# Turning one pair's queries with a DMA transpose and emitting that pair's scores later

## The chip, the cores and the metric

The kernel runs on one core of one Trainium2 chip. The metric is the device time of one execution in microseconds (us); three runs of the kernel before took 225.99, 226.20 and 226.31 us, so the median is 226.2 us.

A core has five engines that run their own instruction streams and wait for each other by semaphores: TensorE (PE in the profile, with its weight loads as PEld), VectorE (DVE), ScalarE (ACT), GpSimd (POOL) and SyncE (SP), which here only issues DMA. TensorE writes to eight banks of PSUM, each of 128 partitions by 512 float32.

## The reference, cut to what matters

```python
def _attn_ref(q, k, v, is_retrieval, n_sink, window):        # 4 batches, 8 heads, 768 tokens, 64 wide
    scores = scale * np.matmul(q, k.transpose(0, 1, 3, 2))
    ...
    stream_keep = causal & (is_sink | in_win)                # 4 sinks, window of 64
    mask = np.where(retr, causal, stream_keep)               # heads 0, 2 and 6: causal; the others: windowed
    a = softmax(np.where(mask, scores, -1e9))
    return np.matmul(a, v)

def reference(...):
    x = attn_out.transpose(0, 2, 1, 3).reshape(B * S, H * D) # 3072 tokens, 512 wide
    h = x @ w_in                                             # 512 x 2048
    g = np.maximum(h, 0.0) + alpha * np.minimum(h, 0.0)
    return g @ w_out                                         # 2048 x 512
```

## The kernel before, in words

**Tiles.** The heads go in four pairs per batch, `PAIRS = [(2, 6), (1, 5), (0, 4), (3, 7)]`, and the pairs of all batches are numbered n = 0 to 15; batch 1 has 4 to 7. Pair 4 has two full heads (`RETR`), pairs 5 and 7 two windowed ones, pair 6 one of each (head 0 full, head 4 windowed). Each pair's queries lie transposed in `qT` (64 rows for each head of the pair, 768 columns), its keys in `kT`.

**Steps.** Everything the kernel does is cut into named steps, and one table, `ORDER`, gives the order in which they are emitted; each engine runs its own steps in that order. The names:

- `Lq`, `Lk`, `Lv` n: loads of a pair from DRAM, issued by SP. `Cq`, `Ck`, `Cv`: casts to bf16 on ACT, DVE or POOL.
- `Tq`, `Tk` n: six 128x128 transposes on TensorE into a bank (L377); `tq`, `tk`: their copies out of PSUM, on ACT (L382 for the queries).
- `Dq`, `Dk` n: the same turn as a DMA transpose issued by SP (L335 for queries); before, only for pairs 8 to 15.
- `S`n.h.m: the scores of piece m of head h (0 or 1) of pair n. A full head has six pieces of 448 columns, a windowed one three of 352, 352 and 448. `s`: the exponential on ACT (L485 full, L557 and L559 windowed), which frees the bank. `m`: the mask on DVE.
- `A`n.h: probabilities times values on TensorE (L595); `a`: division on DVE (L605, L606). `X`n: the pair's output turned into `xT` by a DMA transpose on SP (L614).
- `P`t.f: the first matmul of a stretch t of tokens (L640); `p`, `g`: its activation on ACT and DVE. `O`t.s.u: a quarter (four matmuls, L660) of the second; `o`: its copy out on ACT (L666) and its store from POOL. Stretches 0 and 1 are batch 0, 2 and 3 batch 1, so that batch 0's second matmul runs while batch 1's attention does.
- `near`i: resets of a buffer for windowed probabilities, on DVE.

**Scores side by side.** From pair 4 on, `S` steps are only collected, in `burst`, and `emit_burst` writes them out when the next step comes that isn't allowed beside them (`beside_burst`). If both halves (first heads and second heads) have at least `SPLIT = 576` columns, matmuls of the two halves are interleaved, each on its own 64 rows of the array (L446), and run at the same time. If not, they go one behind the other on all 128 rows (L439).

**Banks.** `take` gives a step the bank that was freed longest ago in the order of emission, `give` returns it. The choice is fixed when the program is written; when the program runs, TensorE waits until that bank has really been read out.

**DMA.** SP's DMAs run in order on one queue, and each waits for a semaphore that the eighth one before it used. The rows of `q` are loaded with `row_tokens(n)` tokens in a piece: 6 for n < 8, so that one load brings 128 x 2 rows of 1536 bytes (L212), and 1 from n = 8 on, which makes two loads of 128 x 6 rows of 256 bytes (L215). With 6 the columns come out of the transpose permuted, and `put_q` puts them in order while it copies; the DMA transpose can't, and needs 1.

Of the kernel before, what the change touches and what calls it, by code (L numbers as in the profile page):

```python
# [34 lines left out]
m6.1.1 s7.1.2 m6.1.0 s7.0.2 m7.0.2 S6.0.4 S6.0.2 S4.1.2 S6.1.2 S6.0.0 s4.1.2 s6.0.4 m4.1.1 s6.0.1 s6.1.2 O1.0.1 m6.0.5
m7.1.0 m4.1.4 m7.1.2 m6.1.2 S6.0.3 A4.1 s6.0.0 m6.0.0 m6.0.1 A7.1 O1.1.2 A6.1 s6.0.3 m6.0.4 m6.0.3 s6.0.2 a4.1 a6.1
A6.0 A7.0 a6.0 O1.1.3 O0.0.0 O0.0.1 O0.0.2 O1.0.2 m10.0.2 O1.0.3 O0.0.3 o0.0 X4 X6 a7.1 a7.0 X7 P2.9 P2.3 p2.9 P3.4
Ck9 Cq9 g2.9 P2.14 p2.14 g2.14 Cq8 p3.4 Lq10 Lq11 Dk8.0 P2.10 p2.10 Dk9.1 o1.0 p2.3 g2.3 g3.4 Dk8.1 P3.2 P3.14 P3.12
P2.8 Dq8 P2.1 P3.8 o1.1 p3.2 Dk9.0 Lv10 g2.10 Dq9 p3.14 P2.7 Ck10 g3.2 p3.12 g3.12 g3.14 P2.2 p2.2 g2.2 Cq10 Dq10
P2.11 p2.1 g2.1 p2.11 p2.8 g2.11 P3.6 P2.5 p2.5 g2.5 P2.13 p2.13 g2.8 g2.13 P2.0 p2.0 g2.0 p2.7 P3.0 p3.0 P2.4 S8.0.5  # L40
Lv8 Lv11 P2.15 P2.12 s8.0.5 Cq11 g3.0 p2.15 g2.7 g2.15 S8.0.0 p2.12 g2.12 Ck11 p3.6 P2.6 s8.0.0 p2.6 S9.0.2 g3.6 p2.4
g2.4 s9.0.2 g2.6 p3.8 P3.10 g3.8 p3.10 O3.0.0 O2.0.0 S8.1.5 s8.1.5 O3.0.1 O2.0.1 g3.10 m8.0.0 Cv8 S8.1.3 S9.0.0 S8.0.3
S8.0.1 S9.1.0 s8.1.3 s9.1.0 s8.0.1 s9.0.0 s8.0.3 m8.0.3 m8.0.1 O2.0.2 O2.0.3 o2.0 Dk10.1 Lv9 m9.0.0 Cv9 m8.0.5 Dk11.0
m9.1.0 m9.0.2 S8.0.4 S9.1.1 S9.0.1 S8.1.4 S10.1.1 Dq11 s9.1.1 s8.1.4 Lq13 Lk13 O3.0.2 Dk10.0 s10.1.1 s9.0.1 s8.0.4
O3.0.3 o3.0 Dk11.1 S10.1.0 S10.1.2 m9.0.1 S11.0.2 S9.1.2 S8.0.2 S11.0.0 s9.1.2 Cv10 m9.1.1 A9.0 s11.0.2 s10.1.0 O2.3.0
m9.1.2 A9.1 a9.0 a9.1 X9 s10.1.2 s11.0.0 O2.3.1 Lq15 Lv14 Lq12 S8.1.0 S11.0.1 m10.1.0 s8.0.2 S10.0.1 S8.1.2 S10.0.3
S8.1.1 S10.0.0 O2.3.2 s8.1.2 s8.1.0 m8.1.4 Cq13 s11.0.1 s8.1.1 m11.0.2 m8.0.4 m11.0.0 A8.0 s10.0.0 m8.1.5 m10.1.1
O2.3.3 m10.1.2 a8.0 S11.1.2 S10.0.4 S11.1.0 S10.0.2 S10.0.5 m8.1.3 m11.0.1 s10.0.3 s10.0.1 S11.1.1 s10.0.2 s11.1.2
A10.1 s11.1.1 O2.2.0 O2.1.0 s10.0.4 m6.0.2 m10.0.1 Cv11 m8.1.1 m8.1.0 a10.1 m10.0.4 Ck13 m10.0.0 m11.1.2 A11.0 A8.1
O2.1.1 s10.0.5 o2.3 s11.1.0 Dk13.0 m11.1.1 m10.0.3 m10.0.5 m11.1.0 A10.0 a11.0 a8.1 a10.0 O3.1.0 A11.1 Cq12 O2.2.1  # L50
O2.2.2 O2.2.3 a11.1 X8 O2.1.2 O3.1.1 O3.1.2 X10 o2.2 O3.1.3 O2.1.3 X11 P4.11 o2.1 P4.14 P5.14 p5.14 P4.4 P4.6 Lk12
P5.0 g5.14 Ck12 p4.4 p4.6 p4.11 P4.13 g4.6 p4.14 g4.11 Lq14 g4.14 P5.12 P4.5 P4.12 p4.13 Dq12 o3.1 p5.0 g4.13 Cq14
g5.0 Dk13.1 p4.5 g4.5 g4.4 Cv14 P4.9 p4.9 g4.9 P4.2 P5.2 Dq13 p5.12 g5.12 P4.10 p5.2 P4.8 P4.1 p4.12 g4.12 g5.2 p4.10
g4.10 Lv15 Dk12.0 Dk12.1 Lv12 p4.1 Lk14 Lv13 Lk15 g4.1 P4.7 P4.0 p4.2 g4.2 p4.8 g4.8 p4.0 p4.7 g4.7 P4.15 S12.0.5 Cv12
S13.0.1 s13.0.1 S12.0.3 s12.0.5 P4.3 s12.0.3 P5.4 g4.0 p4.3 S12.1.5 S12.0.1 S12.0.0 S13.1.1 s13.1.1 Dq14 g4.3 Cq15
Ck14 m12.0.3 O4.3.0 s12.1.5 s12.0.1 O4.3.1 O4.3.2 s12.0.0 p4.15 g4.15 P5.6 P5.10 S12.1.1 S12.0.4 S12.0.2 p5.4 S13.1.0
g5.4 p5.6 s12.0.4 Dk14.0 P5.8 s13.1.0 s12.0.2 p5.8 s12.1.1 m12.0.0 g5.6 O4.3.3 Ck15 p5.10 g5.8 m12.0.1 g5.10 m12.0.4
O5.1.0 Cv13 O5.1.1 O5.1.2 o4.3 Dk14.1 S14.1.1 S14.0.0 S12.1.4 S14.0.1 S14.1.0 S13.0.2 m12.1.1 s14.1.0 s13.0.2 O4.2.0
m12.0.5 A12.0 s14.0.1 s12.1.4 O5.1.3 Dk15.1 s14.1.1 Dk15.0 s14.0.0 a12.0 m14.0.1 Dq15 o5.1 O4.2.1 S13.1.2 S12.1.2
S14.1.2 S14.0.4 m13.1.0 m14.0.0 m13.0.1 S14.0.5 S13.0.0 O4.2.2 O4.2.3 s13.1.2 m13.1.2 m13.1.1 s13.0.0 s14.0.4 s14.0.5  # L60
m13.0.2 S12.1.0 m12.1.5 s14.1.2 S12.1.3 S15.0.0 S14.0.3 m13.0.0 A13.1 o4.2 s12.1.0 s12.1.2 A13.0 s15.0.0 O5.0.0
s12.1.3 s14.0.3 m14.0.4 Cv15 a13.1 O5.0.1 a13.0 S15.0.1 S15.0.2 m12.1.0 S15.1.0 S15.1.2 S15.1.1 S14.0.2 O4.1.0 s15.0.2
s15.1.0 m12.1.4 s14.0.2 s15.1.1 m14.1.1 m14.0.5 m14.1.2 m12.1.3 m14.1.0 A12.1 m14.0.3 A14.1 A14.0 s15.1.2 m15.0.0
m15.0.2 m15.1.0 s15.0.1 m15.1.1 O4.1.1 X13 m15.1.2 m15.0.1 a14.0 a14.1 A15.0 A15.1 a12.1 O4.0.0 X14 O4.0.1 O4.0.2
O4.0.3 X12 o4.0 a15.0 O4.1.2 a15.1 O4.1.3 X15 o4.1 O5.0.2 O5.0.3 o5.0 P6.11 p6.11 P6.2 P6.15 P6.10 p6.10 P7.4 P6.0
P6.1 g6.11 g6.10 p6.1 P6.6 P7.8 p6.15 g6.15 g6.1 p6.0 g6.0 P6.5 p7.4 p6.5 p6.6 g7.4 g6.6 g6.5 P6.3 P6.12 P7.2 p6.3
p6.12 g6.12 p6.2 g6.2 P6.4 p7.8 P7.6 P6.14 g6.3 g7.8 p7.6 p6.4 g7.6 g6.4 P7.10 P6.7 P6.8 p6.8 p6.7 P7.0 P6.9 P6.13
g6.7 p7.2 g7.2 g6.8 p7.10 g7.10 p6.9 P7.14 O6.3.0 P7.12 p6.13 g6.13 p7.12 O6.0.0 O6.0.1 O6.1.0 p7.0 g7.0 g6.9 O6.3.1
O7.0.0 O6.3.2 O6.1.1 p7.14 p6.14 g6.14 g7.12 O6.3.3 o6.3 O6.0.2 O6.1.2 O6.1.3 o6.1 O6.0.3 o6.0 O6.2.0 O6.2.1 O6.2.2
# [5 lines left out]
def kernel(  # L75
# [293 lines left out]
    def to_array(key, nat, choices, first_half=False):  # L369

        held[key] = take(*choices)
        tr = bank_bf(held[key][0])
        for i in range(6):
            if first_half:
                nc.tensor.transpose(tr[0:D, 128 * i:128 * (i + 1)], nat[:, i, 0:D], ident)
            else:
                nc.tensor.transpose(tr[:, 128 * i:128 * (i + 1)], nat[:, i, :], ident)  # L377
# [520 lines left out]
```

## Time and profile before

| | |
|---|---|
| median of 3 runs | 226.2 us (225.99 to 226.31) |
| profiled execution, its own time | 226.88 us |
| its span, first to last instruction | 225.2 us |
| granted TensorE clock | 1.000 |
| batch 1's scores and sums | about 56.7 to 74.3 us |
| first matmul of batch 1 begins | 80.3 us |
| HBM read, written | 27.71 MB, 6.29 MB |

A group's line on the page names the line of the program, the engine, the operation, what it writes and reads, the count, busy time and mean; behind the second bar stands the idle time of the engine just before, with what ended most of it. The chain that ended last is followed back from the last instruction: at each step to what released it, or to the instruction before it on its engine. In its order of time a row is start, length and what ran. In the timeline a row is start, length, engine, line and operation, with the engine's idle time before it in brackets. SPq rows are the issue of a DMA on SP, not its transfer.

### The profile page before, as it was taken

To read this page: it belongs to the slowest core of one execution; us is meant where nothing else is said; L and a number is where in the kernel's file an instruction comes from. 1 tells how busy PE (TensorE), PEld (TensorE's weight loads), DVE (VectorE), ACT (ScalarE), POOL (GpSimd) and SP (SyncE) were. 2 spreads that over 40 slices of the span, in tenths; PEclk is the share of its full clock that TensorE was granted. 3 is DMA by queue.
4 is the path that set the end of the run, shared out by engine and by line. 5 is a ranking of instruction groups with operands and counts; after the bars stand their busy time and mean duration, and the time that the engine had idled before them with its cause. 6 is when DMAs were issued, how large, how long until landed. Compare 5 with 4: busy or idle time off the path is not lost.

```text
span 225.2 us, 5132 instructions
## 1 busy us (share of the span) xinstructions
PE 218.4 (97%) x1934; PEld 133.8 (59%) x1962; DVE 149.8 (67%) x403; ACT 141.8 (63%) x289; POOL 43.0 (19%) x88
## 2 busy tenths in 40 slices
PE   7999999999999999999999999999999999999995
...
GB/s 198 316 232 202 250 209 286 220 196 235 181 291 187 172 206 251 172 212 186 226 115 228 168 271 182 230 143 113 129 95 39 152 96 0 0 1 3 89 64 127
DMA packets 96185, 37.58 MB, mean 167 GB/s; under 512 B 83208, under 2 KB 94368, under 8 KB 96160
## 3 DMA queue, kind: packets, MB, share of 16 engines
...
q10 hardware_dynamic: 464, 0.40, 0.5%
...
HBM read 27.71 MB, written 6.29 MB: 151 GB/s over the span
## 4 chain that ended last, share of the span: by engine, by line
PE 83%; DMA 7%; SPq 5%; POOL 2%; issue 1%; DVE 0%; DVEq 0%
PE P L660 35%; PE P L640 34%; DMA kf<-in_k_dram 7%; PE P L595 5%; PE P L446 4%; SPq L228 3%; SPq L212 2%; PE P L679 2%; PE P L439 1%; PE P L377 1%; POOL w_in_b L736 1%; POOL vb L357 1%; SPq L251 0%; POOL g L341 0%; POOL g L328 0%
## 5 line engine op out<-in xcount | busy, mean ns | idle before, releaser
L652 DVE SCALAR_TENSOR_TENSOR g<-neg,oma,P 128x256 bf16<-128x256 f32 (+1 forms) x128 | 70.9, 610 | 41.0 <-ACT neg L645 40.6
L640 PE MATMUL P<-xT,w_in_b 128*128 128x256 bf16 (+1 forms) x501 | 86.0, 325 | 0.6 <-issue 0.2
L660 PE MATMUL P<-w_out_b,g 128*128 128x512 bf16 x351 | 82.8, 379 | 1.1 <-issue 0.3
L645 ACT ACTIVATE neg<-P 128x512 f32<-128x512 f32 x96 | 54.4, 601 | 25.1 <-PE P L640 17.1
L640 PEld LDWEIGHTS <-w_in_b 128*128 128x128 bf16 x512 | 49.4, 98 | 32.5 <-DVE g L652 0.2
L660 PEld LDWEIGHTS <-g 128*128 128x128 bf16 x368 | 34.1, 98 | 37.5 <-issue 1.3
L485 ACT ACTIVATE eR<-P 128x448 bf16<-128x448 f32 (+3 forms) x63 | 35.7, 613 | 5.6 <-PE P L446 3.2
L666 ACT COPY ot<-P 128x512 f32<-128x512 f32 x23 | 13.7, 597 | 36.1 <-PE P L660 30.6
L670 POOL DMA_DIRECT2D out_dram<-ot x18 | 10.3, 573 | 108.0 <-ACT ot L666 107.8
L557 ACT ACTIVATE eS<-P 128x352 bf16<-128x352 f32 x45 | 20.6, 481 | 4.3 <-PE P L446 3.4
L606 DVE TENSOR_TENSOR xn<-P,rcp 128x448 bf16<-128x448 f32 (+1 forms) x32 | 19.0, 595 | 1.1
L568 DVE TENSOR_TENSOR eS<-eS,ms_near 128x352 bf16<-128x352 bf16 x45 | 14.6, 337 | 1.3 <-ACT eS L557 1.1
L494 DVE TENSOR_TENSOR eR<-eR,mr_near 128x128 bf16<-128x128 bf16 x54 | 10.5, 225 | 4.5 <-ACT eR L485 4.3
L595 PEld LDWEIGHTS <-eS 128*128 128x128 bf16 x266 | 9.8, 97 | 3.1 <-issue 1.2
L595 PE MATMUL P<-vb,eS 128*128 128x65 bf16 x266 | 11.2, 193 | 0.5 <-DVE vb L357 0.2
L446 PE MATMUL P<-qT,kT 64*128 64x176 bf16 (+7 forms) x167 | 10.6, 250 | 0.0
L446 PEld LDWEIGHTS <-kT 64*128 64x128 bf16 x167 | 6.8, 94 | 6.1 <-issue 5.5
L605 DVE RECIPROCAL rcp<-P 128x7 f32<-128x7 f32 (+1 forms) x32 | 6.2, 192 | 5.6 <-PE P L595 5.0
L688 DVE COPY ot<-P 128x128 f32<-128x128 f32 x1 | 0.3, 292 | 14.3 <-PE P L679 14.3
L595 PE MATMUL P<-vb,eR 128*128 128x65 bf16 x258 | 9.8, 193 | 0.0
L595 PEld LDWEIGHTS <-eR 128*128 128x128 bf16 x258 | 9.1, 97 | 1.0
L429 PE MATMUL P<-qT,kT 128*128 128x192 bf16 (+19 forms) x54 | 8.7, 255 | 0.2
...
## 6 DMA issues: line engine op xcount, KB each, us to landing
...
```

The source lines that it names most:

```text
L446: nc.tensor.matmul(to, keys[own], queries[own], start=True, stop=True)
L485: nc.scalar.activation(ebuf[n, hh][:, lo:hi].rearrange("p (x c) -> p x c", x=len(parts)), P[:, got[0]:got[0] + len(parts), 0:(hi - lo) // ...
L494: nc.vector.tensor_tensor(ej, ej, mr_near, op=ALU.mult)
L557: nc.scalar.activation(slots, sc[:, 0:352].rearrange("p (s c) -> p s c", c=176), AF.Exp, scale=scale)
L568: nc.vector.tensor_tensor(slots, slots, ms_near[:, 0:2, :] if m == 0 else ms_near[:, 1:3, :], op=ALU.mult)
L595: nc.tensor.matmul(pav[:, i, :], e[:, o:o + 128], vv[:, j, hh, 0:D + 1], start=(m == 0), stop=(m == len(terms) - 1))
L606: nc.vector.tensor_tensor(xn[n][:, 0:nt, D * hh:D * hh + D], pav[:, :, 0:D], rcp.to_broadcast([128, nt, D]), op=ALU.mult)
L640: nc.tensor.matmul(psg[:, w * i:w * (i + 1)], w_in_b[:, c, 128 * fb:128 * (fb + 1)], xT[:, c, o:o + w], start=(x == 0), stop=(x == 3))
L645: nc.scalar.activation(neg[t, f], bank(held["P", t, f][0]), AF.Relu, scale=-1.0)
L652: nc.vector.scalar_tensor_tensor(g_buf[t % 2][:, fb, 0:w], neg[t, f][:, c], oma[:, fb:fb + 1], bank(got[0])[:, c], op0=ALU.mult, op1=ALU.add)
L660: nc.tensor.matmul(bank(held["O", t, s][0]), g_buf[t % 2][:, f, 128 * s:128 * (s + 1)], w_out_b[:, f, :], start=(f == 0), stop=(f == 15))
L666: nc.scalar.copy(ot, bank(got[0]))
```

## The change

Pair 7's queries are turned by DMA. `row_tokens(7)` becomes 1 for the queries, so that Lq7 is two loads of 256-byte rows; the steps Tq7 (TensorE) and tq7 (ACT) are gone; Dq7 (SP) stands where Tq7 stood. The table `ORDER` is rewritten between about the 280th and the 425th of its 1081 steps: S6.1.1, S6.0.5, S4.1.1, S4.1.3 and S4.1.5 stand ahead of the first scores of pair 7 in separate groups, S4.0.3 and S4.1.0 are in other groups than before, S6.1.0 has moved behind S7.0.1, and Cv7 is earlier; Ck7.0 and m5.0.1 have moved by a few places.

```diff
@@ the table, two of its lines
-m4.0.4 s4.1.0 m4.1.0 m5.0.2 O0.1.3 s5.1.2 O0.3.0 O0.2.3 Cq7 m5.1.2 Ck8 Tq7 near1 A5.1 o0.1 S6.1.0 S4.0.3 s4.1.4 s6.1.0
+s4.0.0 m5.1.1 m4.0.4 m5.0.2 O0.1.3 s5.1.2 O0.3.0 O0.2.3 Cq7 m5.1.2 Ck8 Dq7 near1 A5.1 o0.1 S4.1.0 s4.1.4 O0.3.1 a5.1
...
     CROSS = 8
+    TURNED = (7,)
...
     def row_tokens(n, h=None):
 
-        return 1 if n >= CROSS else 6 if h is None or RETR[h] else 2
+        return 1 if n >= CROSS or h is None and n in TURNED else 6 if h is None or RETR[h] else 2
...
             if n:
                 two = [(4,), (5,)] if n < 4 else ANY
-                item(f"Tq{n}", lambda n=n, two=two: to_array(("q", n), natq[n], two))
-                item(f"tq{n}", put_q, ("q", n), n, slice(0, 128), TQ[n])
+                if n in TURNED:
+                    item(f"Dq{n}", dma_q, n)
+                else:
+                    item(f"Tq{n}", lambda n=n, two=two: to_array(("q", n), natq[n], two))
+                    item(f"tq{n}", put_q, ("q", n), n, slice(0, 128), TQ[n])
```

The step that takes its place, from the kernel before:

```python
    def dma_q(n):
        nc.sync.dma_start(qT[n % NK][:, 0:S].rearrange("p (i r) -> p i r", r=128),
                          natq[n].rearrange("p i c -> p (i c)"), transpose=True)
```

The groups of scores that the rewritten stretch makes, with the columns of the first and of the second heads:

| before | columns | now | columns |
|---|---|---|---|
| S4.0.4 S4.0.0 S5.1.2 S4.0.5 S4.1.4 S4.1.0 | 1344, 1344 | S4.0.4 S4.0.0 S5.1.2 S4.0.5 S6.1.1 S4.0.3 | 1792, 800 |
| | | S4.1.4 | 0, 448 |
| S6.1.0 S4.0.3 | 448, 352 | S4.1.0 | 0, 448 |
| | | S6.0.5 S4.1.5 S4.1.3 S4.1.1 | 448, 1344 |
| S7.0.0 S6.0.5 S7.1.1 S4.1.1 S4.1.3 S7.0.1 | 1152, 1248 | S7.0.0 S7.1.1 S7.0.1 S6.1.0 | 704, 704 |
| S7.1.0 S7.0.2 S4.1.5 S6.0.1 S7.1.2 S6.1.1 | 896, 1600 | S7.1.0 S7.0.2 S6.0.1 S7.1.2 | 896, 800 |

**SP, from Lq7 to the loads behind pair 4's values.** `qf_76` is the buffer of Lq7, `kf_77` that of Lk8, `vf_83` and `vf_81` those of Lv7 and Lv4, `kf_78` that of Lk9. Before:

```order
L212 DMA qf_76<-in_q_dram 128x2x384 [waits DMAHW1_49]
L251 DMA kf_77<-in_k_dram 128x6x64 [waits DMAHW2_49,DVE_49]
L251 DMA kf_77<-in_k_dram 128x6x64 [waits DMAHW3_49]
L251 DMA vf_83<-in_v_dram 128x6x64 [waits DMAHW4_49,Pool_49]
L244 DMA vf_83<-in_v_dram 112x7x64 [waits DMAHW5_49,Pool_49]
L247 DMA vf_83<-in_v_dram 4x7x64 [waits DMAHW6_49]
L251 DMA vf_81<-in_v_dram 128x6x64 [waits DMAHW7_49]
L251 DMA vf_81<-in_v_dram 128x6x64 [waits DMAHW0_49]
L244 DMA kf_78<-in_k_dram 112x7x64 [waits DMAHW1_49,Pool_49]
```

Now:

```order
L216 DMA qf_76<-in_q_dram 128x6x64 [waits DMAHW1_49]
L216 DMA qf_76<-in_q_dram 128x6x64 [waits DMAHW2_49]
L252 DMA kf_77<-in_k_dram 128x6x64 [waits DMAHW3_49,DVE_49]
L252 DMA kf_77<-in_k_dram 128x6x64 [waits DMAHW4_49]
L252 DMA vf_83<-in_v_dram 128x6x64 [waits DMAHW5_49,Pool_49]
L245 DMA vf_83<-in_v_dram 112x7x64 [waits DMAHW6_49,Pool_49]
L248 DMA vf_83<-in_v_dram 4x7x64 [waits DMAHW7_49]
L252 DMA vf_81<-in_v_dram 128x6x64 [waits DMAHW0_49]
L252 DMA vf_81<-in_v_dram 128x6x64 [waits DMAHW1_49]
L336 DMA_TRANSPOSE qT<-natq_91 128x6x128 [waits DMAHW2_49,PE_49,Activation_49]
L245 DMA kf_78<-in_k_dram 112x7x64 [waits DMAHW3_49,Pool_49]
```

Lq7 has become two DMAs, and the transpose, which waits for Cq7 on ACT, stands between Lv4 and Lk9; everything behind it on SP waits with it.

**ACT, from the last copy of keys on.** Before:

```order
L485 ACTIVATE eR<-P 128x448 [waits DVE_49,PE_49]
L485 ACTIVATE eR<-P 128x448 [waits PE_49] x2
L557 ACTIVATE eS<-P 128x2x176
L559 ACTIVATE eS<-P 128x96
L328 CAST natq_91<-qf_76 128x2x6x64 [waits DMAHW1_49]
L666 COPY ot<-P 128x512 [waits PE_49]
L485 ACTIVATE eR<-P 128x448
L557 ACTIVATE eS<-P 128x2x176 [waits DVE_49,PE_49]
L485 ACTIVATE eR<-P 128x448
L485 ACTIVATE eR<-P 128x448 [waits PE_49]
L382 COPY qT<-P 128x768
```

Now:

```order
L558 ACTIVATE eS<-P 128x2x176 [waits DVE_49,PE_49]
L486 ACTIVATE eR<-P 128x448 x2
L558 ACTIVATE eS<-P 128x2x176
L560 ACTIVATE eS<-P 128x96
L329 CAST natq_91<-qf_76 128x2x6x64 [waits DMAHW2_49,DMAHW1_49]
L667 COPY ot<-P 128x512 [waits PE_49]
L486 ACTIVATE eR<-P 128x448
L486 ACTIVATE eR<-P 128x448 [waits PE_49]
L486 ACTIVATE eR<-P 128x448
L486 ACTIVATE eR<-P 128x448 [waits DVE_49]
L486 ACTIVATE eR<-P 128x448 [waits PE_49]
L486 ACTIVATE eR<-P 128x448 [waits DVE_49,PE_49]
```

The exponential of S6.1.1 has come to the front, that of S6.1.0 (with its wait for DVE) has left the stretch, and the copy of the queries is gone. Cq7, the cast of `natq_91`, has one exponential of a windowed piece in front of it in place of one of a full piece.

**TensorE, where pair 7's scores begin.** Before, behind the last matmul of O0.3.3:

```order
L660 LDWEIGHTS g_97
L660 MATMUL P<-w_out_b,g_97 128x512
L446 LDWEIGHTS kT
L446 MATMUL P<-qT,kT 128x176 [waits Activation_49]
L446 LDWEIGHTS kT
L446 MATMUL P<-qT,kT 128x176 [waits DVE_49]
```

Now, the last matmul of O0.3.3 and the first of pair 7's scores:

```order
L661 LDWEIGHTS g_97
L661 MATMUL P<-w_out_b,g_97 128x512
L447 LDWEIGHTS kT [waits DMAHW2_49]
L447 MATMUL P<-qT,kT 128x176 [waits Activation_49]
L447 LDWEIGHTS kT
L447 MATMUL P<-qT,kT 128x176 [waits Activation_49]
```

and, one quarter earlier, the end of the four pieces that go in file:

```order
L440 LDWEIGHTS kT
L440 MATMUL P<-qT,kT 128x64 [waits DVE_49]
L440 LDWEIGHTS kT
L440 MATMUL P<-qT,kT 128x384
L440 LDWEIGHTS kT
L440 MATMUL P<-qT,kT 128x320 [waits Activation_49]
L440 LDWEIGHTS kT
L440 MATMUL P<-qT,kT 128x128
L661 LDWEIGHTS g_97
L661 MATMUL P<-w_out_b,g_97 128x512
```

The scores of pair 7 now wait for a DMA (the transpose) where they waited for the copy on ACT, and the group ahead of them, which runs in file, is new.

More of the change, by code (lines that the diff above doesn't have):

```diff
@@ L26 @@
 p0.11 wo0 g0.8 p0.14 g0.14 Lv5 wo1 wo2 wo3 P1.8 p1.8 S5.0.0 P0.7 p0.12 g1.8 kz3 nz1 m4.1.2 g0.12 P0.6 Ck6.1 P0.4.0 Lq7
-P0.4.1 Lk8 Ck6.0 s5.0.0 p0.7 S5.0.2 s5.0.2 Cq4 Tq4 tq4 g0.11 P0.4.2 P0.9 Ck7.1 Ck7.0 S5.1.0 p0.9 g0.9 P1.4 s5.1.0 p1.4
+P0.4.1 Lk8 Ck6.0 s5.0.0 p0.7 S5.0.2 s5.0.2 Cq4 Tq4 tq4 g0.11 P0.4.2 P0.9 Ck7.1 S5.1.0 p0.9 g0.9 P1.4 s5.1.0 p1.4 Ck7.0
 Lv6 S4.0.1 Cq6 m12.1.2 P0.5.0 s4.0.1 P0.5.1 P0.5.2 P1.12 m5.0.0 g1.4 g0.7 p0.4 p0.5 m5.1.0 g0.4 g0.5 Cv5 P1.10 S5.0.1
-p1.10 s5.0.1 near0 p0.6 g0.6 O0.1.0 Tq6 Tk6 tk6.1 tk6.0 O0.2.0 P1.6 p1.6 m5.0.1 Tk7 tk7.1 Lv4 S4.0.2 O0.2.1 g1.6 ro1
@@ L30 @@
-tq6 p1.12 s4.0.2 tk7.0 O0.1.1 O0.2.2 O0.1.2 g1.10 S4.0.4 S4.0.0 S5.1.2 g1.12 S4.0.5 S4.1.4 S4.1.0 s4.0.4 s4.0.0 m5.1.1
-m4.0.4 s4.1.0 m4.1.0 m5.0.2 O0.1.3 s5.1.2 O0.3.0 O0.2.3 Cq7 m5.1.2 Ck8 Tq7 near1 A5.1 o0.1 S6.1.0 S4.0.3 s4.1.4 s6.1.0
-O0.3.1 a5.1 s4.0.5 s4.0.3 O0.3.2 O0.3.3 m4.0.1 m4.0.5 Cv4 m4.0.3 tq7 S7.0.0 S6.0.5 S7.1.1 S4.1.1 Lk9 Lk10 Lq9 o0.2
-o0.3 S4.1.3 S7.0.1 A5.0 s4.1.1 s7.0.0 m4.0.0 a5.0 X5 A4.0 s7.0.1 Lk11 s7.1.1 a4.0 s4.1.3 O1.1.0 Cv7 s6.0.5 m7.0.0
-m7.1.1 Lq8 S7.1.0 S7.0.2 S4.1.5 m4.1.3 S6.0.1 S7.1.2 S6.1.1 O1.1.1 Cv6 s7.1.0 O1.0.0 s4.1.5 m7.0.1 s6.1.1 m4.1.5
@@ L35 @@
[L35 to L69, printed above, removed]
@@ L70 @@
-O7.0.1 O7.0.2 O6.2.3 o6.2 m12.0.2 g7.14 L2 l2 O7.0.3 o7.0 L0 L1 l1 warm1 l0
+p1.10 s5.0.1 near0 p0.6 g0.6 O0.1.0 Tq6 Tk6 tk6.1 tk6.0 O0.2.0 P1.6 m5.0.1 p1.6 Tk7 tk7.1 Lv4 S4.0.2 O0.2.1 g1.6 ro1
+tq6 p1.12 s4.0.2 tk7.0 O0.1.1 O0.2.2 O0.1.2 g1.10 S4.0.4 S4.0.0 S5.1.2 g1.12 S4.0.5 S6.1.1 S4.0.3 s6.1.1 S4.1.4 s4.0.4
+s4.0.0 m5.1.1 m4.0.4 m5.0.2 O0.1.3 s5.1.2 O0.3.0 O0.2.3 Cq7 m5.1.2 Ck8 Dq7 near1 A5.1 o0.1 S4.1.0 s4.1.4 O0.3.1 a5.1
+s4.1.0 s4.0.5 s4.0.3 m4.1.0 O0.3.2 S6.0.5 S4.1.5 S4.1.3 S4.1.1 O0.3.3 m4.0.1 m4.0.5 Cv4 s4.1.5 m4.0.3 s4.1.3 S7.0.0
@@ new lines @@
+Lk9 Lk10 Lq9 o0.2 o0.3 S7.1.1 S7.0.1 S6.1.0 A5.0 s4.1.1 s7.0.0 s6.1.0 Cv7 m4.0.0 a5.0 X5 A4.0 s7.0.1 Lk11 s7.1.1 a4.0
+O1.1.0 s6.0.5 m7.0.0 m7.1.1 Lq8 S7.1.0 S7.0.2 m4.1.3 S6.0.1 S7.1.2 O1.1.1 Cv6 s7.1.0 O1.0.0 m7.0.1 m4.1.5 m6.1.1
+s7.1.2 m6.1.0 s7.0.2 m7.0.2 S6.0.4 S6.0.2 S4.1.2 S6.1.2 S6.0.0 s4.1.2 s6.0.4 m4.1.1 s6.0.1 s6.1.2 O1.0.1 m6.0.5 m7.1.0
+m4.1.4 m7.1.2 m6.1.2 S6.0.3 A4.1 s6.0.0 m6.0.0 m6.0.1 A7.1 O1.1.2 A6.1 s6.0.3 m6.0.4 m6.0.3 s6.0.2 a4.1 a6.1 A6.0 A7.0
+a6.0 O1.1.3 O0.0.0 O0.0.1 O0.0.2 O1.0.2 m10.0.2 O1.0.3 O0.0.3 o0.0 X4 X6 a7.1 a7.0 X7 P2.9 P2.3 p2.9 P3.4 Ck9 Cq9 g2.9
@@ new lines @@
+P2.14 p2.14 g2.14 Cq8 p3.4 Lq10 Lq11 Dk8.0 P2.10 p2.10 Dk9.1 o1.0 p2.3 g2.3 g3.4 Dk8.1 P3.2 P3.14 P3.12 P2.8 Dq8 P2.1
+P3.8 o1.1 p3.2 Dk9.0 Lv10 g2.10 Dq9 p3.14 P2.7 Ck10 g3.2 p3.12 g3.12 g3.14 P2.2 p2.2 g2.2 Cq10 Dq10 P2.11 p2.1 g2.1
+p2.11 p2.8 g2.11 P3.6 P2.5 p2.5 g2.5 P2.13 p2.13 g2.8 g2.13 P2.0 p2.0 g2.0 p2.7 P3.0 p3.0 P2.4 S8.0.5 Lv8 Lv11 P2.15
+P2.12 s8.0.5 Cq11 g3.0 p2.15 g2.7 g2.15 S8.0.0 p2.12 g2.12 Ck11 p3.6 P2.6 s8.0.0 p2.6 S9.0.2 g3.6 p2.4 g2.4 s9.0.2
+g2.6 p3.8 P3.10 g3.8 p3.10 O3.0.0 O2.0.0 S8.1.5 s8.1.5 O3.0.1 O2.0.1 g3.10 m8.0.0 Cv8 S8.1.3 S9.0.0 S8.0.3 S8.0.1
@@ new lines @@
+S9.1.0 s8.1.3 s9.1.0 s8.0.1 s9.0.0 s8.0.3 m8.0.3 m8.0.1 O2.0.2 O2.0.3 o2.0 Dk10.1 Lv9 m9.0.0 Cv9 m8.0.5 Dk11.0 m9.1.0
+m9.0.2 S8.0.4 S9.1.1 S9.0.1 S8.1.4 S10.1.1 Dq11 s9.1.1 s8.1.4 Lq13 Lk13 O3.0.2 Dk10.0 s10.1.1 s9.0.1 s8.0.4 O3.0.3
+o3.0 Dk11.1 S10.1.0 S10.1.2 m9.0.1 S11.0.2 S9.1.2 S8.0.2 S11.0.0 s9.1.2 Cv10 m9.1.1 A9.0 s11.0.2 s10.1.0 O2.3.0 m9.1.2
+A9.1 a9.0 a9.1 X9 s10.1.2 s11.0.0 O2.3.1 Lq15 Lv14 Lq12 S8.1.0 S11.0.1 m10.1.0 s8.0.2 S10.0.1 S8.1.2 S10.0.3 S8.1.1
+S10.0.0 O2.3.2 s8.1.2 s8.1.0 m8.1.4 Cq13 s11.0.1 s8.1.1 m11.0.2 m8.0.4 m11.0.0 A8.0 s10.0.0 m8.1.5 m10.1.1 O2.3.3
```

23 lines of the change are left out of this document (added).

## The prediction

> **What bounds the kernel now.** I read the page first: busy time, the slices, the chain that ended last. Then I read the chain in order of time for the stage that the change touches, and the waits of TensorE alone.
>
> ```profile
> PE 218.4 (97%) x1934; PEld 133.8 (59%) x1962; DVE 149.8 (67%) x403; ACT 141.8 (63%) x289; POOL 43.0 (19%) x88
> PE   7999999999999999999999999999999999999995
> PE 83%; DMA 7%; SPq 5%; POOL 2%; issue 1%; DVE 0%; DVEq 0%
> PE P L660 <- issue: 0.3, 2, 0.2
> ```
>
> TensorE is busy in every slice but the first and the last. The last row is the whole answer of its waits from 40 us to the end: it waited for nobody, and stood 0.3 us in all. So the time after 40 us is TensorE's own work, and a microsecond of new waiting there is a microsecond of kernel. The stage of the change, as the chain has it:
>
> ```profile
> 56.77 0.68 PE P L446 x9
> 57.45 2.70 PE P L660 x12
> 60.15 0.34 PE P L377 x6
> 60.48 0.39 PE P L595 x13
> 60.87 0.34 PE P L439 x4
> 61.22 0.05 issue
> 61.27 2.54 PE P L660 x11
> 63.81 0.60 PE P L446 x10
> 64.41 1.18 PE P L595 x34
> ...
> 66.45 0.80 PE P L446 x14
> ...
> 70.72 0.19 PE P L439 x2
> ...
> 80.32 1.76 PE P L640 x8
> ```
>
> L446 rows are scores of two heads side by side (64 rows of the array each), L439 rows scores in file, L377 the six transposes of Tq7, L660 the second matmul, L595 the attention's sums. At 80.32 the first matmul of batch 1 begins; it needs the output of X7.
>
> **TensorE's own work.** A piece of a full head has 448 columns, one of a windowed head 352, 352 and 448. Before, the groups were 1344 and 1344 columns side by side (0.68), 800 in file (0.34), 1152 beside 1248 (0.60), 1600 beside 896 (0.80): 2.42 us, and Tq7 0.34, together 2.76. S6.0.3, alone, is the row at 70.72: 448 columns in 0.19, or 0.424 ns a column. Now the groups are 1792 beside 800 (0.68 + 0.19 = 0.87); S4.1.4 alone (0.19); S4.1.0 alone (0.19); S6.0.5 with S4.1.5, S4.1.3 and S4.1.1, where the smaller side has 448 columns, under SPLIT, so that all 1792 go in file (0.76); 704 beside 704 (0.68 - 0.27 = 0.41); 896 beside 800 (0.80 - 0.30 = 0.50). That is 2.92 us. **Net +0.16 us**: what the transposes gave up is lost in pairing.
>
> **A bank that has to come free.** At S4.1.4 all eight banks are held: S4.0.4, S4.0.0, S5.1.2, S4.0.5, S4.0.3, the sums O0.1 and O0.2, and S6.1.1, whose exponential alone is emitted before it. So S4.1.4 waits for that exponential.
>
> ```profile
> 57.10 1.42 ACT L485 ACTIVATE eR<-P 128x448 bf16<-128x448 f32 x3 [0.16 <-PE P L446]
> 58.39 0.48 ACT L557 ACTIVATE eS<-P 128x352 bf16<-128x352 f32 x1
> 61.20 0.47 ACT L557 ACTIVATE eS<-P 128x352 bf16<-128x352 f32 x1 [0.54 <-DVE rcp L605]
> 62.41 0.82 ACT L382 COPY qT<-P 128x768 bf16<-128x768 bf16 x1
> 63.09 1.34 ACT L666 COPY ot<-P 128x512 f32<-128x512 f32 x2
> ```
>
> ACT could take its first score at 57.10, 0.33 us after the group began. S6.1.1 comes later in its group, at 57.3 to 57.5; with 0.48 the bank is free at 57.8 to 58.0, and TensorE is there at 56.77 + 0.87 = 57.64. I take **+0.30 us**; the ends are 0, if the records' drain isn't waited for, and 0.40. Everything else on ACT gets easier: the 0.82 of tq7 goes, and S6.1.0's exponential, which waited 0.54, now comes later.
>
> **The transpose by DMA.** These rows carry Dq7's time.
>
> ```profile
> 48.45 4.24 SPq L212 DMA_DIRECT2D qf<-in_q_dram  x1
> 59.55 0.97 SPq L251 DMA_DIRECT2D vf<-in_v_dram  x2
> 60.62 0.49 SPq L244 DMA_DIRECT2D kf<-in_k_dram  x1
> 66.59 2.98 SPq L614 DMA_TRANSPOSE xT<-xn  x1
> 71.55 0.44 SPq L247 DMA_DIRECT2D kf<-in_k_dram  x1
> 72.50 0.99 SPq L215 DMA_DIRECT2D qf<-in_q_dram  x2
> 73.59 4.82 SPq L614 DMA_TRANSPOSE xT<-xn  x3
> L335 SPq DMA_TRANSPOSE qT<-natq x8: 1214/1222/1631, 85.7 to 158.0; - x8
> 58.87 0.86 ACT L328 CAST natq<-qf 128x768 bf16<-128x768 f32 x1
> 60.28 0.63 DVE L347 CAST natk<-kf 128x896 bf16<-128x896 f32 x1 [0.57 <-DMA kf<-in_k_dram]
> 63.41 0.94 POOL L362 CAST vb<-vf 128x896 bf16<-128x896 f32 x1 [2.33 <-DMA vf<-in_v_dram]
> 57.00:59.00 2.00, 2.00 (x18) 1.00 (x14) 0.68 (x3) 1.90 (x6) 0.94 (x1) 1.00 0.53 121
> 62.00:66.00 4.00, 3.95 (x58) 2.39 (x58) 1.64 (x7) 3.88 (x10) 1.97 (x3) 1.00 1.11 272
> ```
>
> Lq7 becomes two loads in rows of 256 bytes where it was one in rows of 1536. Lk8, which is two such loads of 256-byte rows and as many bytes, came in at 60.28 after Lq7 had come in by 58.87: 1.41 us. So the finer Lq7 costs between 0 and 1.41 us more; as the DMA engines were half idle at 57 to 59 (share 0.53), I take 0.4. Cq7 starts 0.2 to 0.4 later than its 58.87 anyway, as the first exponential ahead of it on ACT is now that of S6.1.1 (from 57.3 to 57.5, in place of 57.10), so that this delay is mostly covered there. On DVE the cast of Lk8, at 60.28, moves by 0.4, and behind it the reset of a score buffer and A5.1's output; no TensorE row reads these before 64.8.
> The Trainium skill's DMA: Bandwidth & Descriptors (Specifications) asks for transfers of at least 512 bytes for full rate. If that halved the rate the 0.4 would be 0.7, and the forecast 227.4; no row here has both sizes undisturbed.
>
> Dq7 stands behind the loads of Lv4, whose issue ended at 60.52; one more load issue (0.49) makes that 61.0. Its least landing is 61.0 + 1.22 (the bare issue) = 62.2. Its most is 61.0 + 2.98 (X5's issue, in an equally full queue) + 2.56 = 66.5, where 2.56 is the longest that X7 can have taken after its issue: that ended at 78.41, and its reader, the fourth matmul after 80.32, stood at 80.97 unstalled. In between, Lv4's data arrived at 63.41 and Dq7's stand behind them: 63.41 + 0.4 + 1.22 = **65.0**, which I take.
>
> TensorE comes to S7.0.0 at 57.64 + 0.30 + 0.19 + 2.70 (three quarters of sums) + 0.39 + 0.19 + 1.73 (eight matmuls of 0.216, from twelve between 61.22 and 63.81) + 0.76 + 0.86 = 64.76. So it waits **0.24 us**, from 0 to 1.74. A4.0 next needs the bank of O0.3: that sum ends just before, and ACT must copy two banks out (1.34) behind two exponentials; I add **0.10**, from 0 to 0.4.
>
> **The X transposes.** Behind Dq7 on SP wait Lk9, Lk10, Lq9, X5, Lk11, Lq8, X4, X6 and X7. SP gets 0.49 + 1.22 to 2.98 longer, 1.7 to 3.5, and gives back up to 1.76 of X5's issue (2.98 against 1.22 bare) and the half us in which it stood still from 71.99 to 72.50. X7's reader is itself 0.8 later. The worst left is 0.4 us, if X7 has no slack; the best is 0. I take **0.10**. The loads behind are cast after 76 us and need no price.
>
> **Sum**: 0.16 + 0.30 + 0.24 + 0.10 + 0.10 = +0.90 us. The profiled execution took 226.88 (span 225.2, 1.7 around it), so it would be 227.8; it lies 0.7 above the median of 226.2, on whose scale the forecast is **227.1 us**.
>
> **Rivals.** *The DMA path decides.* Dq7 lands at 66.5: 0.16 + 0.30 + 1.74 and 0.4 at X7 make +2.6, **228.8**. For it speak the full DMA (share 1.11 at 62 to 66) and X5's 2.98; against it that the qT transposes issued in 1.22 in the median. It takes over when Dq7 lands after 65.6. Chance 0.20.
>
> *Not slower: ACT is relieved.* ACT gives up 0.82 and a wait of 0.54 just where TensorE needs banks. If S6.1.1's exponential is through by 57.64 and Dq7 lands before 64.5, only 0.16 is left: **226.4**, within 0.2% of before. The point is Dq7 ahead of TensorE. Against it: the eight held banks. Chance 0.20.
>
> *Faster: the transposes cost more than the chain shows.*
>
> ```profile
> L377 PE MATMUL P<-ident,natq 128*128 128x128 bf16 x6 | 0.5, 219 | 0.0
> ```
>
> If each of the six held TensorE for its 219 ns, 1.31 us would go instead of 0.34; with the waits gone, 0.16 - 0.97 = -0.8, **225.4**. Against it: the next matmul stands 0.34 after the first transpose. Chance 0.10.
> The Trainium skill's TensorE: Matmul & The Clock Gate (Part 4, PE-mode transpose) gives about 275 ns for such a transpose; six would be 1.65, an estimate by that page, and this rival 225.1. The chain's 0.34 for six contradicts it as a price of throughput.
>
> **How the numbers follow.** The forecast has 0.50 (its own range 226.7 to 227.7). A measurement of this kernel can tell about 0.2%, 0.45 us. Slower: 0.50 + 0.20 = 0.70; same 0.20; faster 0.10. The range leaves out the fastest tenth and some of the slow end: 226.2 to 228.8.
>
> **What would show it.** In the chain after: L440 and L447 rows of 2.9 us in this stage; a short wait of TensorE on ACT near 57.7; one on the DMA of qT at S7.0.0 near 64.8; the first matmul of batch 1 near 81.2. Wrong would be: no wait of TensorE at all (then the time is 226.4), a wait over 1 us at S7.0.0 or at the first matmul, or a gain.

## The result and the profile after

The changed kernel is slower, by somewhat more than was forecast.

| | before | changed |
|---|---|---|
| median | 226.33 us (225.49 to 227.66, 13 runs) | 228.06 us (227.12 to 229.51, 13 runs) |
| ratio | | 1.0072, 95% interval 1.0051 to 1.0092 |
| profiled execution, its own time | 226.88 us | 227.12 us |
| its span | 225.2 us | 225.4 us |

The ratio times 226.3 is +1.63 us, with an interval of +1.15 to +2.08. The profiled execution is the fastest of the changed kernel's 13, 0.9 below their median, so it doesn't show the whole price. Its page, busy time and slices:

```profile
PE 220.0 (98%) x1956; PEld 133.6 (59%) x1956; DVE 149.4 (66%) x403; ACT 141.1 (63%) x288; POOL 43.0 (19%) x88
PE   7999999999999999999999999999999999999994
```

The waits of TensorE from 40 us on, and the chain that ended last in the order of time, from the first group of the stage:

```profile
PE P L440 <- ACT eS L558: 0.2, 1, 0.2
```

```profile
56.19 0.52 PE P L447 x6
...
56.72 0.47 ACT eS L558
...
57.24 0.35 PE P L440 x2
57.59 2.59 PE P L661 x12
...
63.26 0.86 PE P L661 x4
64.12 0.41 PE P L447 x8
64.53 1.26 PE P L596 x34
...
80.23 17.34 PE P L641 x108
```

Before, nothing but TensorE stood in this part of the chain; now the exponential of S6.1.1 (L558) does, and TensorE waits for it once, 0.2 us at S4.1.4. The pair's scores follow the sums at 64.12 without a wait for the turned queries, and batch 1's first matmul comes 24.04 us after the first group (80.23 - 56.19), where it was 23.55 (80.32 - 56.77). So **+0.49 us** in an execution in which the DMA was in time. I count from the stage's first row since what lies before it differs from one execution to the next: in the profiles of this case the stage begins between 55.70 and 58.20 us (here 0.58 earlier than before, 56.19 against 56.77). What lies behind batch 1's first matmul hardly differs: up to the last copy on DVE it takes 141.94 us here and 141.98 before.

A second profile of the same kernel, of an execution of 228.18 us, shows what the faster one didn't. Its waits of TensorE from 40 us on, and its chain:

```profile
PE P L447 <- DMA qT<-natq: 1.0, 1, 1.0
PE P L440 <- ACT eS L558: 0.2, 1, 0.2
```

```profile
56.10 0.51 PE P L447 x6
...
58.47 0.71 ACT natq L329
59.19 0.05 ACT ot L667
59.24 5.72 DMA qT<-natq
...
65.00 0.48 PE P L447 x8
65.48 1.13 PE P L596 x34
...
81.05 3.03 PE P L641 x18
```

The chain now runs through the turn: Cq7 ends, Dq7 is issued at 59.24, its data are there 5.72 later, at 64.96, and TensorE, there a microsecond earlier, begins pair 7's scores at 65.00. From first group to batch 1's first matmul it is 24.95 us, 1.40 more than before: the 0.49 and one wait of 1.0, less about 0.1 (the sums behind the wait take 1.13 us in place of 1.26). Why the same transpose, issued at the same time, came 5.72 later here and in time there stands in the rows of SP's issues and of the windows. First the faster execution, then the slower one (the issues of Lq7, Lk8 and the turn, the stretch behind it, and the cast of pair 4's values, Cv4, on POOL):

```profile
47.06 3.30 SPq L216 DMA_DIRECT2D qf<-in_q_dram  x2
50.45 3.72 SPq L252 DMA_DIRECT2D kf<-in_k_dram  x2
...
59.29 1.31 SPq L336 DMA_TRANSPOSE qT<-natq  x1
...
59.00:62.00 3.00, 3.00 (x27) 1.60 (x26) 1.99 (x10) 2.41 (x6) 1.51 (x2) 1.00 0.67 151
...
60.61 0.95 POOL L363 CAST vb<-vf 128x896 bf16<-128x896 f32 x1
```

```profile
48.43 3.30 SPq L216 DMA_DIRECT2D qf<-in_q_dram  x2
51.83 4.62 SPq L252 DMA_DIRECT2D kf<-in_k_dram  x2
...
59.24 1.45 SPq L336 DMA_TRANSPOSE qT<-natq  x1
...
59.00:62.00 3.00, 3.00 (x27) 1.57 (x25) 1.94 (x10) 2.41 (x6) 0.57 (x1) 1.00 1.19 235
...
62.98 0.94 POOL L363 CAST vb<-vf 128x896 bf16<-128x896 f32 x1 [2.45 <-DMA vf<-in_v_dram]
```

In a row of the windows the last two numbers are the busy share of the DMA engines and GB/s. In the slower execution the loads ahead of the turn were issued 1.4 us later (48.43 against 47.06), though TensorE was as early (56.10 against 56.19), and at 59 to 62 us the DMA engines were still full (1.19 against 0.67). Cv4 shows the last of these loads, Lv4: in the faster execution its data were there when Cv4 began at 60.61; in the slower one Cv4 waited for them until 62.98, and the turn landed 1.98 behind them. The two other profiles in which TensorE waits for the turn (among the experiments on the X transposes) have the same picture: Cv4 at 62.73 and 62.86, the turn at 64.88 and 65.14. Why SP came to these loads later in one execution than in the other isn't shown.

### The profile page after: what moved, and what is told of

The parts are those of the page before. It is cut to its first block, busy times and chain, and to the rows that moved or that the text cites. A ratio compares the mean times of both kernels' runs of the same rounds, so it can differ in the third digit from the quotient of the medians.

```text
span 225.4 us, 5148 instructions
## 1 busy us (share of the span) xinstructions
PE 220.0 (98%) x1956; PEld 133.6 (59%) x1956; DVE 149.4 (66%) x403; ACT 141.1 (63%) x288; POOL 43.0 (19%) x88
## 4 chain that ended last, share of the span: by engine, by line
PE 89%; DVE 5%; DMA 2%; SPq 1%; issue 0%; POOL 0%; ACT 0%; DVEq 0%
PE P L641 36%; PE P L661 36%; PE P L596 6%; PE P L447 4%; PE P L378 2%; DMA kf<-in_k_dram 2%; PE P L440 2%; PE P L680 2%; DVE xn L607 1%; PE P L430 1%; DVE eS L544 1%; DVE kT L403 1%; POOL g L342 0%; DVE kT L409 0%; DVE xT L626 0%
## 5 line engine op out<-in xcount | busy, mean ns | idle before, releaser
L641 PE MATMUL P<-xT,w_in_b 128*128 128x512 bf16 (+1 forms) x512 | 86.8, 326 | 0.0
L661 PE MATMUL P<-w_out_b,g 128*128 128x512 bf16 x368 | 85.2, 379 | 0.0
L558 ACT ACTIVATE eS<-P 128x352 bf16<-128x352 f32 x45 | 20.7, 493 | 4.2 <-PE P L447 3.8
```

The source lines that it names most:

```text
L558: nc.scalar.activation(slots, sc[:, 0:352].rearrange("p (s c) -> p s c", c=176), AF.Exp, scale=scale)
L641: nc.tensor.matmul(psg[:, w * i:w * (i + 1)], w_in_b[:, c, 128 * fb:128 * (fb + 1)], xT[:, c, o:o + w], start=(x == 0), stop=(x == 3))
L661: nc.tensor.matmul(bank(held["O", t, s][0]), g_buf[t % 2][:, f, 128 * s:128 * (s + 1)], w_out_b[:, f, :], start=(f == 0), stop=(f == 15))
```

## The experiments

All were timed in five rounds beside the kernel before on the same chip, four kernels on each of three chips, in the order told here (before: 226.68, 226.71 and 226.24 us). Microseconds behind a ratio are the ratio less one times 226.3. The theories of the expectations: **A**, TensorE's wait for Dq7 at S7.0.0 decides; **B**, the new order of scores; **C**, the finer load of Lq7; **D**, the turn holds up SP's queue, so that the X transposes come late for batch 1's first matmul; **E**, in the last four, the turn costs in a way that neither place shows.

**The changed kernel again**, unchanged.

> The changed kernel once more, for a second trace and more times. Theory A (the turn's arrival decides: DMA in front of Dq7 arrives at times that differ by microseconds from one execution to the next, and TensorE waits at S7.0.0 in the late ones): ratio 1.005 to 1.009, and if this profiled execution takes over 228 us, a wait of TensorE on the DMA of qT of 1 us or more stands in its chain near 64 us. Rival B (the new order itself, by banks and pairing): the same ratio, no wait on the DMA, and the loss spread over waits on ACT. Rival C (the finer load delays the loads behind it): waits on Lk8 or on Lv4's cast.

228.25 us (227.69 to 228.89), ratio 1.0078 (1.0047 to 1.0109): the same as the first time. Its profile is the second one above.

**The order alone**, with the turn back on TensorE and ACT:

```diff
-    TURNED = (7,)
+    TURNED = ()
@@ the table
- Ck8 Dq7 near1 ... s4.0.3 m4.1.0
+ Ck8 Tq7 near1 ... s4.0.3 tq7 m4.1.0
```

> The new order, but pair 7's queries are loaded in 1536-byte rows and turned on TensorE as before (Tq7 where Dq7 stands, tq7 behind s4.0.3). A: 2.92 + 0.34 - 2.76 = 0.50 of work and 0.30 for the bank, +0.8 us, ratio 1.0035 (1.002 to 1.005). B: the loss stays and Tq7's 0.34 comes on top, ratio 1.008 or more. C: as A.

227.17 us, ratio 1.0037 (1.0013 to 1.0060), +0.84 us. Its only wait after 40 us is the 0.2 for the exponential. The prediction's terms for this kernel are 0.16 + 0.34 (the transposes stay) + 0.30 = 0.80. Its stage is 0.83 longer than before (80.74 - 56.36 = 24.38). B costs what was predicted of it, and that is half of the loss of 1.63. The other half, 0.79, is the turn's; as the turn also saves Tq7's 0.34, it costs about 1.13 in this order.

**The turn alone**: the kernel before, with Dq7 where Tq7 stood.

```diff
+    TURNED = (7,)
@@ the table of the kernel before
- Ck8 Tq7 near1 ... m4.0.3 tq7 S7.0.0
+ Ck8 Dq7 near1 ... m4.0.3 S7.0.0
```

> The order before, with Dq7 in place of Tq7 and without tq7 (and the finer load that it needs). TensorE comes to S7.0.0 at 63.8 - 0.34 = 63.5, about a microsecond earlier than in the changed kernel. A: waits of 1 us and more for the turn, ratio 1.005 to 1.012. B: the turn costs nothing and 0.34 is saved, ratio 0.997 to 0.9995. C: 1.003 to 1.006, without a wait for the turn.

228.95 us (227.09 to 231.23), ratio 1.0087 (1.0054 to 1.0120), +1.97 us, although Tq7's 0.34 is saved: the turn costs about 2.3 here. The two halves of the change, +0.84 and +1.97, add to more than the +1.63 of both. The new order brings TensorE to pair 7's scores later, 7.93 us behind the stage's first row (64.12 - 56.19) against 6.70 here (63.01 - 56.31), which would cover part of the turn's lateness. The profiled execution, again the fastest, had no wait at S7.0.0 but one of 0.2 for an X transpose at batch 1's first matmul. It lies 1.9 below the median, so it doesn't hold what this kernel loses:

```profile
PE P L641 <- DMA xT<-xn: 0.2, 1, 0.2
```

```profile
73.87 4.65 SPq L615 DMA_TRANSPOSE xT<-xn  x3
...
76.53 3.84 DMA xT<-xn
...
80.41 3.62 PE P L641 x20
```

The last X transpose was issued at 76.53 and landed 3.84 later. The three issues end at 78.52, where it was 78.41 before. (The chain puts a load and a cast of later queries ahead of this transpose, but it reads only `xn`, which they don't write; that they held it up isn't shown.)

**The finer load alone**: the kernel before, with Lq7 in rows of 256 bytes and Tq7 kept.

```diff
+    TURNED = (7,)
...
-                item(f"Tq{n}", ...)
+                if False:
+                    item(f"Dq{n}", dma_q, n)
+                else:
+                    item(f"Tq{n}", ...)
```

> The order before and the turn on TensorE; only Lq7 is two loads of 256-byte rows (and tq7 copies straight). A and B: within 0.15% of before, 0.9985 to 1.0015. C: 1.003 or more.

226.39 us, ratio 0.9993 (0.9969 to 1.0018). C is out. The profiled execution was the slowest of the twelve, 228.26 us, without a wait of TensorE after 40 us and with a stage as long as before (81.76 - 58.20 = 23.56): what it loses lies ahead of the stage.

**A turn that nobody reads**: the changed kernel, with Dq7 written to a spare tile, while Tq7 and tq7 turn the queries that are used.

```diff
-                    item(f"Dq{n}", dma_q, n)
-                else:
-                    item(f"Tq{n}", ...)
-                    item(f"tq{n}", put_q, ...)
+                    item(f"Dq{n}", dma_spare, n)
+                item(f"Tq{n}", ...)
+                item(f"tq{n}", put_q, ...)
```

> The new order, the fine load and Dq7 at its place, but Dq7 writes to a spare tile that nobody reads, and pair 7's queries are turned on TensorE (Tq7 behind Dq7, tq7 behind s4.0.3). All DMA is that of the changed kernel; only TensorE's wait for the turn is gone. Theory A (the wait at S7.0.0 is what the order alone doesn't explain): as the order alone, ratio 1.002 to 1.005. Rival D (the turn holds up SP, so that the X transposes or the loads come late): 1.006 or more, with a wait for xT at the first matmul of batch 1.

228.86 us (227.33 to 231.50), ratio 1.0080 (1.0051 to 1.0108), +1.81 us. Against the order alone that is 0.97 more, with nobody waiting for the result (the two intervals just overlap), and so most of the 1.13 that the turn costs where it is read. A can't explain it. Its profiled execution, at 227.79 the second fastest of eight, shows no DMA wait of TensorE, and its stage is as long as the order alone's (80.88 - 56.51 = 24.37), so where the price falls isn't seen.

**Pair 7's first scores later**: the changed kernel, with the group S7.0.0 S7.1.1 S7.0.1 S6.1.0 put behind A5.0 and A4.0, so that TensorE has 1.03 us of sums to do before it needs the queries.

```diff
@@ the table
-S7.0.0 Lk9 Lk10 Lq9 o0.2 o0.3 S7.1.1 S7.0.1 S6.1.0 A5.0 s4.1.1 s7.0.0 s6.1.0 ... X5 A4.0
+Lk9 Lk10 Lq9 o0.2 o0.3 A5.0 s4.1.1 ... X5 A4.0 S7.0.0 S7.1.1 S7.0.1 S6.1.0 s7.0.0 s6.1.0
```

> The changed kernel with pair 7's first group of scores (S7.0.0, S7.1.1, S7.0.1, S6.1.0) behind A5.0 and A4.0, 1.26 us of TensorE's work later. A: up to 1.26 us of each wait is covered: ratio 1.002 to 1.005 and no wait, or one under 0.5 us, for the turn. D: no change, 1.006 or more.

227.43 us, ratio 1.0041 (1.0017 to 1.0066), +0.93 us: 0.7 to 0.8 less than the changed kernel, as A has it, and the best of the kernels with the turn. What is left is more than the new order costs without the transposes (0.84 - 0.34 = 0.50), though the interval, +0.38 to +1.49, reaches down to that and also overlaps the changed kernel's. The profiled execution, 227.41 us, is close to the median, and its stage is 0.38 longer than before (80.46 - 56.53 = 23.93). In its chain the sums stand where the wait stood:

```profile
63.60 0.86 PE P L661 x4
64.47 1.03 PE P L596 x34
65.50 0.41 PE P L447 x8
```

**The turn earlier on SP**: Dq7 ahead of the loads of Lv6 (the section on the change names the buffer `vf_83` as that of Lv7; it is Lv6's).

```diff
@@ the table, SP's steps in it
-Lk8 Lv6 Lv4 Dq7
+Lk8 Lv4 Dq7 Lv6
```

> The changed kernel with Lv4 ahead of Lv6 and Lv6 behind Dq7 on SP, so that two loads of 192 KB and 196 KB fewer stand in front of the turn; it should land 1.0 to 1.5 us earlier. A: most of the wait goes, ratio 1.002 to 1.005. D: no gain, 1.006 or more.

228.13 us, ratio 1.0061 (1.0042 to 1.0080), +1.38 us. The wait at S7.0.0 is gone from the trace, and another has come, for X7 at batch 1's first matmuls:

```profile
PE P L641 <- DMA xT<-xn: 0.4, 2, 0.2
```

```profile
74.45 5.80 SPq L615 DMA_TRANSPOSE xT<-xn  x3
```

Before, the same three issues took 73.59 to 78.41, in the changed kernel's second profile 74.49 to 78.40; here they end at 80.25. This is D's place: in this trace, time that S7.0.0 no longer loses is partly lost there. By its time, the kernel can't be told from the changed one.

**The same in the order of before**: the turn alone, with Lk8 Lv4 Dq7 Lv6 on SP.

```diff
@@ the table of the turn alone, SP's steps in it
-Lk8 Lv6 Lv4 Dq7
+Lk8 Lv4 Dq7 Lv6
```

> The order before with Dq7 for Tq7 and without tq7, and the loads as in the kernel with the earlier turn. TensorE comes to S7.0.0 a microsecond earlier than in the changed kernel (63.0 against 64.1 in the two traces). A: a part of the wait stays, 1.000 to 1.005, below the 1.0087 of the turn alone; if the turn were in time, 0.9985. D: 1.006 or more.

228.39 us (226.72 to 231.11), ratio 1.0070 (1.0036 to 1.0103). The profiled execution was the fastest, 1.7 below the median and without a wait for DMA, so the trace doesn't hold what this kernel loses, and the time doesn't tell A from D. The trace does show what a turn that comes in time is worth: the stage takes 23.22 us (79.61 - 56.39), 0.33 less than before, which is Tq7's 0.34.

**The X transposes earlier**, four kernels: the loads Lk11 and Lq8, which the casts Ck11 and Cq8 read after batch 1's first matmuls have begun, put behind X7 on SP's queue, in the changed kernel, in that with the unread turn, in the kernel before (the control) and in that with the turn alone.

```diff
@@ the table, SP's steps in it
-X5 Lk11 Lq8 X4 X6 X7
+X5 X4 X6 X7 Lk11 Lq8
```

> The changed kernel with the loads Lk11 and Lq8, which are read only after batch 1's first matmuls, put behind X7 on SP's queue, so that the X transposes stand directly behind X5. If the turn's cost is that it pushes the X transposes back on the queue (D): the ratio falls from 1.007 to about 1.004 (what the new order costs alone), and no wait for xT at the first matmul of batch 1. If its cost is the wait for the queries at S7.0.0 (A): nothing changes, 1.007. If the turn disturbs the executions in a way that neither place shows (E): 1.007 to 1.008, with no wait in the profiled execution.

> The kernel in which the turn by DMA goes to a tile that nobody reads (it took 1.008 times as long as before), with the same two loads behind X7. D: 1.004. A gave 1.004 for the unread turn already, and has nothing to say on these loads. E: stays near 1.008.

> The kernel before with the same two loads behind X7, and nothing else: the control. D, with no turn on the queue and X7 almost without slack there: 0.998 to 1.000. A and E: 1.000. Above 1.001 would mean that the move of the loads has a price of its own, to be taken off the two others.

> The kernel before with only the turn by DMA (its own order of scores; that took 1.0087), and the two loads behind X7. D: the turn's queueing is gone and Tq7's 0.34 us are saved, 0.9985 to 1.001, perhaps better than both. A, whose wait is longer in this order as TensorE comes to S7.0.0 at about 63.0: 1.006 to 1.009. E: 1.007 to 1.009.

| | median | ratio to before | over the control |
|---|---|---|---|
| kernel before, loads moved | 230.37 us | 1.0181 (1.0137 to 1.0226) | |
| changed kernel, loads moved | 231.93 us | 1.0245 (1.0198 to 1.0291) | 1.0063 |
| unread turn, loads moved | 231.88 us | 1.0243 (1.0198 to 1.0288) | 1.0061 |
| turn alone, loads moved | 232.55 us | 1.0278 (1.0233 to 1.0324) | 1.0095 |

All four expectations missed: the move costs 4.1 us by itself. That I had thought these loads free was wrong. The control's one wait of TensorE after 40 us, the SP rows, and two rows of DVE:

```profile
PE P L640 <- DVE g L652: 2.5, 1, 2.5
```

```profile
64.88 12.36 SPq L614 DMA_TRANSPOSE xT<-xn  x4
...
79.36 4.92 SPq L215 DMA_DIRECT2D qf<-in_q_dram  x6
84.38 4.60 SPq L351 DMA_TRANSPOSE kT<-natk  x3
```

```profile
91.58 0.63 DVE L347 CAST natk<-kf 128x896 bf16<-128x896 f32 x1 [4.04 <-issue]
92.12 3.09 DVE L652 SCALAR_TENSOR_TENSOR g<-neg,oma,P 128x256 bf16<-128x256 f32 x7
```

The same cast in the changed kernel with the loads moved:

```profile
94.40 0.63 DVE L348 CAST natk<-kf 128x896 bf16<-128x896 f32 x1 [5.15 <-DMA kT<-natk]
```

With the loads behind X7, six query loads stand in a row ahead of the key transposes Dk8 and Dk9, which are issued at 84.38 where it was 80.91. A later cast of keys on DVE writes the buffer that such a transpose reads. In the control DVE stands 4.04 us ahead of it, for which the view names no cause; in the changed kernel with the loads moved it stands 5.15, and there the view names the key transpose (before, the cast began at 88.55 without a wait). The activations `g` are queued behind that cast, and TensorE stands 2.5 us for a bank. In its profile none of the three kernels with the turn waited for X7 now, so their first matmul was relieved as D asked, and yet they keep a price: 0.6, 0.6 and 0.95% over the control, where it was 0.72, 0.80 and 0.87% (in the first two of each the new order's 0.37 is included). These differences are rough, as each ratio is known to about 0.45%. So the wait for X7 can't be the whole price; as these kernels have a new wait, though, they don't show where those with the loads in their old place lose it. Two of the three show A's wait. The changed kernel with the loads moved:

```profile
PE P L641 <- DVE g L653: 3.6, 1, 3.6
PE P L447 <- DMA qT<-natq: 1.1, 1, 1.1
PE P L440 <- ACT eS L558: 0.2, 1, 0.2
```

and the turn alone with the loads moved, whose TensorE comes to S7.0.0 sooner:

```profile
PE P L641 <- DVE g L653: 3.4, 1, 3.4
PE P L447 <- DMA qT<-natq: 1.9, 1, 1.9
```

In the third, with the unread turn, the wait behind the key transposes is 3.1 in place of the control's 2.5. Here SP's queue itself is on the path: with the turn the first key transpose is issued 5.47, 5.47 and 5.48 us behind batch 1's first matmul (changed, unread, alone), without it 5.12. So the turn's time on SP counts here whether it is read or not.

No kernel beat the one before; the finer load alone is equal to it.

## Why the prediction was right, and where its sizes were off

**The direction and its reason held.** TensorE was the bound, without a wait after 40 us, and in the two profiles of the changed kernel the stage grew by the new order and by the waits that the change added. That these waits are the whole of the price isn't shown.

**TensorE's own work and the bank, 0.16 + 0.30: right.** The stage is 0.49 longer where the DMA is in time, against 0.46, and the order alone costs 0.84 against 0.80. The last three groups take 0.77, 0.41 and 0.49, where I had 0.76, 0.41 and 0.50. The bank wait itself is 0.2, not 0.30; the rest is that the two matmuls behind it take 0.35 where I had 0.19 for them in a running stream.

**The transpose, 0.24 at S7.0.0: the term that was too small.** It is 1.0 and 1.1 us in two traces of this order, and 0 in the fastest execution. The landing that I took, 65.0, is what those show (64.96 and 64.88), and Dq7 did land behind Lv4's data; that the number fits is luck all the same. Lv4 came 0.8 earlier than in my sum (62.98 against 63.81), and Dq7 1.98 behind it instead of 1.22, though it was issued at 59.24, released by Cq7, and not at 61.0. What failed is the other side: I set this landing against TensorE's arrival of one execution, 64.76. TensorE came at 64.0 (65.00 less the wait of 1.0), as its stage began 0.67 earlier, and the DMA had not become earlier with it. With 1.0 for 0.24, the sum of the first three terms is 1.5, inside the measured 1.15 to 2.08. That doesn't make this wait the cause of the whole difference: a turn that nobody reads costs nearly as much, 0.97 against 1.13.

**O0.3's bank at A4.0, 0.10: not there.** No trace has the wait. **X7, 0.10:** not in the two profiles of the changed kernel; 0.2 and 0.4 in two profiles in which S7.0.0 doesn't wait (the turn alone, the turn earlier), and in no other. A wait at S7.0.0 delays X7's reader too and so should give X7 slack, so that the two would come in each other's place; no run tests this.

**The rivals.** "The DMA path decides" named the right mechanism; its 1.74 at S7.0.0 is an end that only the turn alone with the loads moved reaches (1.9). "Not slower" needed Dq7 ahead of TensorE: the fastest execution had that, and its stage was still 0.49 longer; the second profile didn't. "Faster", by dear transposes, is refuted: where the turn came in time in the order of before, the stage lost 0.33 us with them and not 1.31.

**Of the signs that were named**, the wait on ACT near 57 us was in both profiles, that on the DMA of qT in one, at 64 to 65, and the first matmul of batch 1 near 81.2 came at 80.23 and 81.05. "A wait over 1 us at S7.0.0" would have made the prediction wrong; it was 1.0 in the changed kernel itself, just at that edge.

**What stays open.** The unread turn costs 0.97 us over the order alone, and its one profile, 1.1 below its median, doesn't show where. Four of its eight executions and five of the eleven of the turn alone took over 229 us, against one of the twelve of the order alone, and none of these was profiled. The wait behind the key transposes, which opens when SP runs late, could be the place, but no trace of that kernel with the loads in their old place shows it.
